# Loading two weight matrices by casting GpSimd transfers in an RWKV-6 and SoLU kernel, with a fused weight preparation, paired decay loads and a new instruction order

## The chip, the cores and the metric

The kernel runs on one core of one Trainium2 chip. The metric is device time in microseconds (us) of one execution, taken as the median over the runs. Each comparison below ran both kernels on the same chip in the same rounds. The kernel before has two speeds: of its 45 timed executions, 25 took 150.9 to 154.1 us and 20 took 154.4 to 160.0 us. The second kind is called slow here. Ratios use fast runs only, and the numbers in square brackets after a ratio are its 95% interval.

Engine names are those of the profile. PE is TensorE, PEld its weight loads, DVE is VectorE, ACT is ScalarE, POOL is GpSimd. SP is SyncE, which issues most transfers. The granted clock is the share of its full clock that TensorE was allowed. SBUF is the on-chip memory; the tiles here lie across up to 128 partitions of it, and an address in it is an offset within a partition. A hold is a tiny copy on GpSimd that waits for a given load, so that what GpSimd issues next waits too (in b_part the second hold waited 2.69 us and w_out was asked for right after it, at 19.43 us).

## The reference

Four batches and eight heads of 768 steps with 48 elements go through a linear attention with decay. Its output, 3072 rows of 384, goes through a layer of 1024 hidden units with a softmax-like gate and a layer norm.

```python
for t in range(S):                        # S = 768
    cur = einsum('bhd,bhe->bhde', u[None] * kt, vt)
    y[:, :, t] = einsum('bhd,bhde->bhe', rt, state + cur)
    state = wt[:, :, :, None] * state + einsum('bhd,bhe->bhde', kt, vt)
x = y.transpose(0, 2, 1, 3).reshape(B * S, H * D)   # 3072 x 384
h = x @ w_in                              # 384 -> 1024
solu = h * softmax(h)
ln = (solu - mean) / sqrt(var + 1e-6) * g_ln
return ln @ w_out                         # 1024 -> 384
```

## The kernel before

The rows are worked off in 24 pieces of 128 (6 chunks of time for each of 4 batches). A text called ORDER fixes the order in which every stage of every piece is issued, and with it the program of each engine. A letter after a word chooses the engine (a, v, g for ACT, DVE, GpSimd). An engine runs its instructions in that order, so one that waits holds back all that stand behind it (in b_part below ACT stood 10.50 us before a scaling that began at 25.64 us, and its next exponential began at 27.60 us). In the lines below p, q, dg and dv are steps of the term with u, kp and kr are k and r scaled and then transposed, vb is v cast to bf16, y is the attention's output, and H, e, he and hq are the hidden layer, its exponential, the product of both and its square.

The inputs r, k, v and w arrive as rows of 48 f32 values, 192 bytes:

```python
def stage(i):
    c, b = units[i]
    L = live[i]
    if name in "kr":
        if "k_and_r" not in L:
            L["k_and_r"] = io.tile([C, 2, H, 64], F32, tag="kr_in", name="kr_in")
        t = L["k_and_r"][:, "kr".index(name)]
    else:
        t = io.tile([C, H, 64], F32, tag=name + "_in", name=name + "_in")
    L[name] = t[:, :, :D]                                  # D = 48 of 64
    sp.dma_start(out=L[name], in_=src[b, :, c * C:(c + 1) * C, :].rearrange("h t d -> t h d"))
```

The weights come as f32 on the queue of SyncE, and are then prepared. Since the layer norm subtracts a mean, the kernel subtracts the mean over the hidden units from the scaled w_out once, and needs no mean for each row:

```python
def load_w_in(j):
    sp.dma_start(out=win_f[:, j, :], in_=win_v[:, j, :])
def load_w_out(half):
    part = slice(half * KF // 2, (half + 1) * KF // 2)
    sp.dma_start(out=wout_f[:, part, :], in_=wout_v[:, part, :])
...
def setup_w_in(j, engine):                 # three casts on ACT
    copy(engine, win_sb[:, j, :], win_f[:, j, :])
def setup_gain(f, engine):                 # gw = w_out * g, eight chunks
    ...
def setup_mean():
    m_ps = small.tile([128, DM], F32, tag="s", name="mean_ps")
    for f in range(KF):
        pe.matmul(m_ps, lhsT=mean_w, rhs=gw[:, f, :], start=(f == 0), stop=(f == KF - 1))
def setup_w2(f, engine):                   # eight additions, all on GpSimd
    engine.tensor_add(out=w2[:, f, :DM], in0=gw[:, f, :], in1=mean_sb)
def log_w(i):                              # one log for each piece
    act.activation(out=L["lw"][:, :, :D], in_=L["w"], func=LN)
```

The softmax here doesn't subtract the row's maximum and nothing guards it: scores larger than these inputs give would overflow.

## Time and profile before

| | before |
|---|---|
| time, median of the first 3 runs | 152.49 us |
| span of the profiled execution (itself a slow one) | 155.2 us |
| busy share: PE, DVE, POOL, ACT | 90%, 83%, 79%, 77% |
| landing of one 192 KB input load, median | 3.8 us (w 4.2) |
| landing of w_out | 23.9 us after the start |
| matmuls issued by 50 us | 512 of 2156 |

The prediction below shows how to read the busy line, the slices, the windows and the chain. The list of transfers gives, for each kind, the number, the size and the median time from issue to landing:

```profile
kr_in<-in_k_dram SPq DMA_DIRECT2D x24, 192.0 KB, 3.8
v_in<-in_v_dram SPq DMA_DIRECT2D x24, 192.0 KB, 3.8
```

The transfer view between 5 and 11 us gives the packets that the queues moved and the time that they took, as a share of 16 engines' time. In that stretch nearly all are rows of 192 bytes (the trace has 94 other packets among them, and 81 to 111 in the other kernels below), so a packet is called a row here:

```profile
DMA packets 6177, 1.17 MB, mean 195 GB/s; under 512 B 6177, under 2 KB 6177, under 8 KB 6177
...
q1 hardware_dynamic: 6177, 1.17, 101.1%
```

16 engines for 6 us are 96 engine-us. 96 times 1.011 over 6177 packets gives 15.7 ns for one row of 192 bytes. A share above 100% means that the times of packets on one engine overlap. Then the time of a row says how long it is under way, and the number of rows says how fast they come.

### The profile page before, as it was taken

The page shows a single profiled execution, that of the slowest core. Times are in us where ns is not written, and L with a number is a line of the kernel's source. Part 1 is how long each engine was busy: PE and PEld are TensorE (multiplying, and loading weights), DVE is VectorE, ACT ScalarE, POOL GpSimd, SP SyncE. Part 2 cuts the span into 40 slices and gives each one's busy share as a digit, 9 for nine tenths or more (in the row PEclk, how much of TensorE's full clock was granted, in tenths as well). Part 3 has the DMA queues.
Part 4 walks back from the last instruction along what each step waited for, and adds up shares of the span by engine and source line. Part 5 has one row for each costly group of instructions (what it writes and reads, how often), then busy time and mean ns, then how long its engine had stood idle before and what let it go on. Part 6 is the DMA issues. An engine that isn't in the chain of part 4 may idle for free.

```text
span 155.2 us, 5295 instructions
## 1 busy us (share of the span) xinstructions
PE 140.4 (90%) x2156; PEld 109.7 (71%) x2156; DVE 129.4 (83%) x231; ACT 120.2 (77%) x232; POOL 123.1 (79%) x152
## 2 busy tenths in 40 slices
PE   6877897699999899999999799939999999999993
PEld 2344584477786787888788587737888778889771
DVE  7546738899998898999976989999889999998661
ACT  4456767989898979798989698829899888895742
POOL 3375965997999799999947999977799899976800
PEclk9999999999999999999999999999999999999999
DMA  4999997989999999899796999999989311011013
GB/s 95 201 185 301 380 303 152 213 160 190 208 202 184 204 229 187 194 205 233 154 205 157 218 217 200 228 250 180 215 196 211 100 51 55 2 55 55 18 62 127
DMA packets 104970, 27.09 MB, mean 175 GB/s; under 512 B 100329, under 2 KB 104562, under 8 KB 104946
## 3 DMA queue, kind: packets, MB, share of 16 engines
q1 hardware_dynamic: 104946, 26.75, 76.4%
q8 instruction: 17, 0.28, 0.7%
q14 instruction: 7, 0.06, 0.1%
HBM read 22.03 MB, written 4.72 MB: 172 GB/s over the span
## 4 chain that ended last, share of the span: by engine, by line
PE 50%; DMA 14%; DVE 10%; SPq 8%; POOL 8%; ACT 4%; issue 3%; POOLq 0%; DVEq 0%
PE o_ps L71 18%; PE h_ps L71 13%; SPq L71 8%; DMA kr_in<-in_k_dram 8%; DMA wout_f<-in_moe_w_out_dram 6%; POOL w L71 5%; PE kr_ps L71 5%; PE cum_ps L71 3%; PE m_ps L71 3%; PE y_ps L71 3%; PE s_ps L71 3%; DVE hq L71 3%; DVE kp L71 2%; PE x_ps L71 2%; DVE he L71 1%
## 5 line engine op out<-in xcount | busy, mean ns | idle before, releaser
L71 PE MATMUL o_ps<-w,he 128*128 128x385 bf16 (+2 forms) x200 | 42.2, 315 | 0.3 <-ACT sq L71 0.3
L71 PE MATMUL h_ps<-xT,win_sb 128*128 128x128 bf16 x576 | 36.0, 219 | 0.1
L71 PEld LDWEIGHTS <-win_sb 128*128 128x128 bf16 x576 | 32.9, 98 | 0.9 <-issue 0.2
L71 PE MATMUL o_ps<-inv_col,e 128*128 128x1 bf16 x192 | 31.1, 165 | 0.0
L71 DVE TENSOR_TENSOR he<-h_ps,e 128x1024 bf16<-128x1024 f32 x24 | 29.2, 1217 | 2.2 <-ACT e L71 2.2
L71 POOL TENSOR_TENSOR hq<-he 128x1024 bf16<-128x1024 bf16 x14 | 26.5, 1895 | 3.7 <-DVE he L71 2.4
L71 ACT ACTIVATE e<-h_ps 128x1024 bf16<-128x1024 f32 x24 | 24.5, 1021 | 6.2 <-PE h_ps L71 6.1
L71 PEld LDWEIGHTS <-he 128*128 128x128 bf16 x208 | 19.7, 96 | 10.5 <-issue 0.3
L71 ACT ACTIVATE cum_ps<-cum_ps 128x772 f32<-128x772 f32 (+1 forms) x24 | 19.2, 801 | 8.8 <-PE cum_ps L71 7.6
L71 DVE TENSOR_TENSOR kp<-cum_ps,kr_in 128x768 bf16<-128x768 f32 x24 | 22.7, 948 | 0.6 <-DMA kr_in<-in_r_dram 0.5
L71 POOL TENSOR_TENSOR q<-p,u_bc 128x384 bf16<-128x384 bf16 x23 | 22.0, 962 | 0.6 <-DVE p L71 0.5
L71 POOL TENSOR_TENSOR p<-kr_in 128x384 bf16<-128x384 f32 x18 | 17.9, 1001 | 5.4 <-DMA kr_in<-in_k_dram 5.4
L71 PEld LDWEIGHTS <-kp 128*128 128x128 bf16 x272 | 17.6, 102 | 4.4 <-DVE kp L71 2.3
L71 POOL TENSOR_TENSOR dv<-vb,dg 128x384 bf16<-128x384 bf16 x22 | 18.2, 830 | 2.3 <-ACT vb L71 1.5
L71 DVE TENSOR_TENSOR m<-m_ps,uts 128x1024 bf16<-128x1024 f32 x14 | 17.0, 1223 | 3.1 <-PE m_ps L71 3.0
L71 PEld LDWEIGHTS <-e 128*128 128x128 bf16 x192 | 18.3, 96 | 0.1
L71 PE MATMUL kr_ps<-ident,kp 128*128 128x128 bf16 x192 | 15.9, 230 | 1.4 <-DVE kp L71 1.4
L71 PEld LDWEIGHTS <-kr 64*128 64x128 bf16 (+1 forms) x272 | 10.7, 98 | 4.9 <-DVE kr L71 2.2
L71 ACT ACTIVATE lw<-w_in 128x384 bf16<-128x384 f32 x23 | 11.7, 523 | 2.7 <-DMA w_in<-in_w_dram 2.7
L71 ACT COPY kr<-kr_ps 128x1024 bf16<-128x1024 bf16 x13 | 13.2, 1014 | 0.5 <-PE kr_ps L71 0.4
L71 POOL TENSOR_SCALAR_AFFINE_SELECT m<-m 128x1024 bf16<-128x1024 bf16 x10 | 11.0, 1103 | 2.5 <-ACT m L71 2.4
L71 PE MATMUL cum_ps<-lw,uti_neg 128*128 128x384 bf16 x24 | 8.3, 347 | 4.8 <-DVE kp L71 3.3
(93 smaller groups left out, 284.3 us busy)
## 6 DMA issues: line engine op xcount, KB each, us to landing
w_in<-in_w_dram SPq DMA_DIRECT2D x24, 192.0 KB, 4.2
kr_in<-in_r_dram SPq DMA_DIRECT2D x24, 192.0 KB, 3.8
kr_in<-in_k_dram SPq DMA_DIRECT2D x24, 192.0 KB, 3.8
v_in<-in_v_dram SPq DMA_DIRECT2D x24, 192.0 KB, 3.8
out_dram<-o SPq DMA_DIRECT2D x23, 192.0 KB, 3.1
win_f<-in_moe_w_in_dram SPq DMA_DIRECT2D x3, 512.0 KB, 6.1
wout_f<-in_moe_w_out_dram SPq DMA_DIRECT2D x2, 768.0 KB, 8.8
out_dram<-o SPq DMA_DIRECT2D x2, 96.0 KB, 1.6
```

The lines of the kernel that those rows point to most:

```text
L71: made = make(*args, **kwargs)
```

## The change

The intent is to take work off the compute engines before the first output: GpSimd's transfers cast w_in on the way, each group of weights is held back until a given load has landed so that the first inputs go first, w_out is centred and scaled in one DVE operation for half of it, and w with its log is taken in pairs. The core of the diff:

```diff
 ORDER = """          # all of it replaced; weights as iwin0..2, iwout0..1
+            elif name == "w":
+                if i % 2 == 0:
+                    t2 = io.tile([C, 2, H, 64], F32, tag="w_in", name="w_in", bufs=4)
+                    ...
+                if i >= 4:
+                    sp.dma_start(out=L["w2_in"]..., in_=src[b:b + 2, ...])   # two batches in one
-    win_f = consts.tile([128, KM, DF], F32)
+    win_sb = consts.tile([128, KM, DF], BF16)
-    wout_f = consts.tile([128, KF, DM], F32)
+    wout_f = consts.tile([128, KF, DM], F32R)
+    seen = consts.tile([1, 4], F32)
+    def after(loaded):
+        n_seen.append(1)
+        pool.tensor_copy(out=seen[:, len(n_seen):len(n_seen) + 1], in_=loaded)
     def load_w_in(j):
-        sp.dma_start(out=win_f[:, j, :], in_=win_v[:, j, :])
+        if j == 0:
+            after(live[2]["w"][:1, 0, :1])
+        pool.dma_start(out=win_sb[:, j, :], in_=win_v[:, j, :])
     def load_w_out(half):
+        if half == 0:
+            after(win_sb[:1, 1, :1])
         ...
-        sp.dma_start(out=wout_f[:, part, :], in_=wout_v[:, part, :])
+        pool.dma_start(out=wout_f[:, part, :], in_=wout_v[:, part, :])
-    mean_w = consts.tile([128, 128], BF16)
-    gw = consts.tile([128, KF, DM], BF16)
+    g_wide = consts.tile([128, KF, 128], F32R)
     def setup_mean(half):
+            pe.matmul(live[0]["mean_ps"], lhsT=g_wide[:, f, :], rhs=wout_f[:, f, :], ...)
     def setup_w2(f, engine):
-        engine.tensor_add(out=w2[:, f, :DM], in0=gw[:, f, :], in1=mean_sb)
+        if "scaled" in live[f]:
+            engine.tensor_add(out=w2[:, f, :DM], in0=w2[:, f, :DM], in1=mean_sb)
+        else:
+            engine.scalar_tensor_tensor(out=w2[:, f, :DM], in0=wout_f[:, f, :].bitcast(F32),
+                                        scalar=gr[:, f:f + 1], in1=mean_sb, op0=MULT, op1=ALU.add)
     ...                # pairs of w in log_w, constants set up in another order
```

## The prediction

The forecast's sum: 3 us from 20 to 50 us, 1 us in the first 20 and 1 to 2 us from 85 to 105, together taken as about 5 us off 152.5, so 147.5 us. The fall of GpSimd's busy time to 115 us never had the transfers in it. Rival (b) rests on the one long square in the trace (4.09 us against 0.68), and rival (c) blamed the holds, stacked with a time for each GpSimd transfer.

> **What bounds the kernel now.** I read the page's summary and slices first, then busy time by stage, then the chain of waits, then single tiles. From the page:
>
> ```profile
> PE 140.4 (90%) x2156; PEld 109.7 (71%) x2156; DVE 129.4 (83%) x231; ACT 120.2 (77%) x232; POOL 123.1 (79%) x152
> ...
> PE   6877897699999899999999799939999999999993
> ...
> DMA  4999997989999999899796999999989311011013
> ```
>
> TensorE is the fullest engine, but all four compute engines are above 75%, and the DMA engines are full from about 5 to 120 us. So an average settles nothing; the stages do. The windows view, one row for each stretch that I chose (busy us, and in brackets the number of instructions):
>
> ```profile
> 0.00:20.00 20.00, 15.19 (x105) 8.39 (x105) 12.94 (x47) 11.23 (x14) 11.63 (x23) 1.00 0.92 237
> 20.00:30.00 10.00, 7.75 (x98) 5.74 (x96) 6.91 (x13) 7.79 (x14) 7.06 (x8) 1.00 0.95 213
> 30.00:50.00 20.00, 19.29 (x309) 15.26 (x308) 18.87 (x31) 17.30 (x34) 18.61 (x24) 1.00 0.95 191
> 50.00:85.00 35.00, 34.60 (x603) 28.75 (x601) 30.62 (x50) 31.05 (x65) 30.27 (x44) 1.00 0.94 195
> 85.00:105.00 20.00, 16.23 (x270) 13.12 (x268) 18.32 (x25) 13.99 (x27) 19.02 (x20) 1.00 0.99 223
> 105.00:150.00 45.00, 44.59 (x766) 36.69 (x763) 40.49 (x66) 37.24 (x77) 36.48 (x37) 1.00 0.41 100
> ```
>
> Columns: PE, weight load, DVE, ACT, POOL, granted clock, DMA share, GB/s. The busy time of PE flatters it, so I count matmuls. In 50 to 85 us it does 603 in 35 us, 17.2 a us; 105 to 150 us has 17.0. I take 17.2 as its full pace. What each stage lacks is its length less its count over 17.2: 0 to 20 us lacks 13.9 us, 20 to 30 us lacks 4.3, 30 to 50 us lacks 2.0, 85 to 105 us lacks 4.3. The end (150 to 155.2 us, 21 matmuls) lacks 4.0. So PE is the bound from about 50 us on, and some 28 us are lost, two thirds of them in the first 30 us. A check from the chain view: one batch of 128 rows costs PE h 1.36, o 0.75 and 0.94, kr 0.47, m 0.33, y 0.39, x 0.18, cum 0.41, s 0.34, together 5.17 us; 24 of them are 124 us, and 124 + 28 is 152, near the span of 155.2 us. (The profiled execution was slower than the timed ones, median 152.49 us; I take the shape from the profile and the level from the times.)
>
> The chain in order of time shows what fills the early loss (start, us, what):
>
> ```profile
> 13.97 9.87 DMA wout_f<-in_moe_w_out_dram
> ...
> 23.87 1.12 ACT gw L71 x2
> ...
> 26.31 0.38 ACT mean_sb L71
> 26.69 0.07 issue
> 26.75 7.75 POOL w L71 x8
> ...
> 39.74 4.45 DMA kr_in<-in_k_dram
> ```
>
> The weights arrive at 23.9 us. They are then scaled, averaged on PE, copied, and GpSimd spends 7.75 us adding the mean eight times. Its own p, q and dv queue up behind that. They free the input buffers, so the DMA of k for later batches is issued late, twice 4.5 us in this chain, and the chain gets back to PE only at 53 us.
>
> The late hole (85 to 105 us) has one large cause, seen in DVE's timeline:
>
> ```profile
> 98.25 4.09 DVE L71 TENSOR_TENSOR hq<-he 128x1024 bf16<-128x1024 bf16 x1
> ```
>
> and on PE, at the end of it:
>
> ```profile
> 103.26 0.34 PE L71 MATMUL cum_ps<-lw,uti_neg 128*128 128x384 bf16 x1 [2.71 <-DVE kp L71]
> ```
>
> The same square took 0.68 us at 40.94 us. Here GpSimd ran q, dv and two p back to back beside it (98.18 to 101.78 us), the square ended 0.6 us later, and PE stood 2.71 us behind.
>
> [...]
>
> **The change part by part.** Counts are from the two lists of operations, durations from the groups by form.
> - w_in cast in the transfer: three casts of 1.05 us leave ACT (3.1 us), at 15.7 to 20.0 us. PE began h at 20.06 us, 0.06 us after the last of them, so up to 1 us of this is on the path. Three transfers of GpSimd come instead, and two for w_out. [...]
> - w_out: before, two scalings on GpSimd (2.5 us), four on ACT, two on DVE, and eight additions on GpSimd (7.75 us). After, four scalings on ACT as before, four additions on GpSimd (3.9 us), and on DVE four that scale and add at once (about 0.55 us each as f32 of 384, 2.2 us). The mean no longer waits for the scaling: g is spread into a 128x1024 tile on ACT (about 1.05 us) and multiplies w_out as it is. From landing to the last addition was 34.5 less 23.9, 10.6 us. I expect some 2 us for mean and copy and 4 us for four additions on each of two engines: 6 us, a gain of 4.5 us for GpSimd. [...]
> - The holding back: the weights start only after w of batch 2 and w_out after w_in, so inputs of four batches share the DMA with less. Weights may land 1 to 2 us later than 23.9 us; the bytes of w_out are the same.
> - w in pairs: twenty logs of 0.52 us become ten of about 0.84 us (the slope from 384 to 1024 elements in the casts and logs is 0.82 ns): 2.1 us off ACT. Ten transfers fewer to issue. The rows stay 192 bytes, so the DMA does the same.
> - The order of all work and engines is new as well. Sums: hq GpSimd 14 to 9, ACT 5 to 8, DVE 5 to 7; kr ACT 13 to 7, DVE 11 to 17; v casts on ACT 6 to 2; masks on GpSimd 10 to 12; halvings there 6 to 9. With these, ACT falls by about 5.6 us to 114.6, DVE rises by about 1 us to 130.4, GpSimd falls by about 8 us to 115 [...]. [...]
>
> On the path: of the 4.3 us lacking in 20 to 30 us and the 2.0 in 30 to 50 us I give back 3. In the first 20 us more batches have their inputs early, 1 us. In 85 to 105 us a lighter GpSimd and another order give back 1 to 2 us, by luck as much as by design. Together about 5 us off 152.5.
>
> **Rivals.** (a) DMA takes over: it is already 0.95 full to 105 us, at 195 GB/s with 192-byte rows. If only the DMA sets when batches come, freeing engines moves nothing and the time stays at 151 to 153. For it: the two waits for k in the chain, and 13.9 us lost at the start. Against it: the share falls to 0.41 after 105 us, so the loads finish 30 us before the end and PE is the one behind. (b) [...] DVE now has seven squares, two v casts and four additions [...]. Two more stalls like the one of 3.4 us would cost 5 us and leave 150 to 154. For it, DVE is the second fullest engine; against it, GpSimd has five squares of 1.9 us fewer. (c) Weights arrive too late [...]: landing at 28 us rather than 24 would eat the 4 us, result 151 to 153. (d) The new order fits so well that PE runs closed from 20 us: 20 + 124 less 6 already done + 4 of end = 142.
>
> **Range and chances.** 5 us off gives 147.5 us. (d) sets the low side, 143.5, (a) to (c) the high side, 151.5. Faster by over 2% means under about 149.4: 0.70. One of the rivals holding all of the gain: 0.24. Two of them together: 0.06.
>
> **What would show it.** No win casts on ACT; the last addition to w_out by about 31 us rather than 34.5; 20 to 50 us with more matmuls than the 407 of before; ACT near 115 and GpSimd near 115 us busy; PE from 50 us at 17 a us. It would be wrong if w_out lands after 27 us, if the float32r matmuls take over 0.4 us each, if DVE squares again take 4 us, or if PE waits for k or w after 50 us.

## The result and the profile after

The changed kernel is correct. It takes 162.14 us (median of 4 runs, 161.08 to 163.51) against 152.18 us for the kernel before (4 runs, 150.94 to 152.75). The ratio of fast runs is 1.0643, 95% interval 1.0539 to 1.0748. A ratio is the mean time of one kernel's fast runs over the mean of the other's fast runs of the same rounds, so it isn't quite the ratio of the medians.

The page of the changed kernel, busy times and two rows of the slices:

```profile
PE 141.8 (88%) x2156; PEld 111.3 (69%) x2157; DVE 127.2 (79%) x236; ACT 115.7 (72%) x218; POOL 118.0 (73%) x157
...
PE   6786248996999999989999989699899999999991
...
DMA  4999999999999999999999999999999991111022
...
kr_in<-in_k_dram SPq DMA_DIRECT2D x24, 192.0 KB, 5.1
...
v_in<-in_v_dram SPq DMA_DIRECT2D x24, 192.0 KB, 5.4
```

Every compute engine but PE has less work (predicted for ACT and GpSimd; DVE was to have 1 us more), and the kernel is 6% slower. The DMA row is full for 33 slices of 4.02 us, to about 133 us. Before it was full for 31 slices of 3.88 us, to about 120 us. The loads of 192 KB land in 5.1 and 5.4 us rather than 3.8. The windows view of the changed kernel, with the columns of the prediction (PE, weight load, DVE, ACT, POOL, granted clock, DMA share, GB/s):

```profile
0.00:20.00 20.00, 12.62 (x92) 6.86 (x94) 10.64 (x43) 9.73 (x13) 9.44 (x21) 0.99 1.23 162
20.00:30.00 10.00, 7.26 (x61) 5.54 (x60) 5.80 (x11) 1.21 (x3) 6.20 (x10) 0.51 1.21 220
30.00:50.00 20.00, 17.85 (x268) 14.02 (x266) 18.49 (x29) 16.77 (x30) 15.51 (x16) 1.00 1.23 177
...
85.00:105.00 20.00, 18.15 (x302) 14.64 (x300) 15.48 (x27) 15.98 (x32) 15.79 (x21) 1.00 1.13 184
```

PE has issued 421 matmuls by 50 us (92 + 61 + 268) against 512 before (527 in the fast profile of b_swq below). The DMA share is above 1.1 where it was 0.92 to 0.99, and in three of the four stretches fewer bytes move than before. Between 5 and 11 us, in the transfer view:

```profile
DMA packets 5236, 0.99 MB, mean 165 GB/s; under 512 B 5236, under 2 KB 5236, under 8 KB 5236
...
q1 hardware_dynamic: 5236, 0.99, 152.3%
```

The same kind of row now takes 96 times 1.523 over 5236, 27.9 ns instead of 15.7. Since these times overlap, the pace falls by less: 5236 rows in 6 us instead of 6177, 15% fewer. Over the whole run the mean of all 98304 rows in the trace is 21.3 ns instead of 15.6. The first transfer of GpSimd is issued only at 11.76 us, so it can't be the weights that slow these. The rest of the kernel then waits for inputs, which the chain of waits in order of time shows (start, us, what):

```profile
14.50 8.13 DMA kr_in<-in_r_dram
...
60.59 6.96 DMA kr_in<-in_k_dram
...
91.65 6.63 DMA v_in<-in_v_dram
```

A second thing went further than foreseen. GpSimd's timeline shows when the weights were asked for (start, us, engine, operation, and in brackets the idle time before it):

```profile
11.40 0.41 POOL L72 COPY seen<-w_in 1x1 f32<-1x1 f32 x1 [2.31 <-DMA w_in<-in_w_dram]
...
20.63 0.50 POOL L72 CAST vb<-v_in 128x384 bf16<-128x384 f32 x1 [3.01 <-DMA v_in<-in_v_dram]
21.08 0.59 POOL L72 DMA_DIRECT2D win_sb<-in_moe_w_in_dram  x1
...
22.47 0.18 POOL L72 CAST seen<-win_sb 1x1 f32<-1x1 bf16 x1
22.59 1.57 POOL L72 DMA_DIRECT2D wout_f<-in_moe_w_out_dram  x2
```

The second hold itself (the copy at 22.47 us) waited for nothing. What kept w_out back was the cast of v at 20.63 us, which stood ahead of the third part of w_in, and so of w_out, in GpSimd's own program. The halves of w_out landed 8.0 and 10.0 us after their issue, the second at 33.4 us instead of 23.9.

### The profile page after: what moved, and what is told of

The parts are those of the page before. It is cut to its first block, busy times and chain, and to the rows that moved or that the text cites. A ratio compares the mean times of both kernels' runs of the same rounds, so it can differ in the third digit from the quotient of the medians.

```text
span 160.8 us, 5277 instructions
## 1 busy us (share of the span) xinstructions
PE 141.8 (88%) x2156; PEld 111.3 (69%) x2157; DVE 127.2 (79%) x236; ACT 115.7 (72%) x218; POOL 118.0 (73%) x157
## 4 chain that ended last, share of the span: by engine, by line
PE 48%; DMA 17%; DVE 11%; SPq 10%; issue 4%; ACT 3%; POOL 3%; DVEq 0%; ACTq 0%; POOLq 0%
PE o_ps L72 16%; PE h_ps L72 13%; SPq L72 10%; DMA kr_in<-in_r_dram 5%; DMA kr_in<-in_k_dram 4%; DMA v_in<-in_v_dram 4%; PE kr_ps L72 4%; PE y_ps L72 3%; PE cum_ps L72 3%; DMA out_dram<-o 3%; DVE kp L72 3%; PE m_ps L72 3%; PE s_ps L72 3%; ACT cum_ps L72 2%; PE x_ps L72 2%
## 5 line engine op out<-in xcount | busy, mean ns | idle before, releaser
L72 PE MATMUL h_ps<-xT,win_sb 128*128 128x128 bf16 x576 | 37.3, 224 | 0.3 <-DVE kp L72 0.3
L72 PEld LDWEIGHTS <-win_sb 128*128 128x128 bf16 x576 | 34.1, 100 | 2.0 <-issue 0.9
L72 POOL TENSOR_TENSOR hq<-he 128x1024 bf16<-128x1024 bf16 x9 | 17.0, 1892 | 9.9 <-DVE he L72 8.7
L72 POOL TENSOR_TENSOR q<-p,u_bc 128x384 bf16<-128x384 bf16 x23 | 21.8, 951 | 1.6 <-DVE p L72 1.0
L72 POOL TENSOR_TENSOR p<-kr_in 128x384 bf16<-128x384 f32 x20 | 19.9, 1000 | 4.0 <-DMA kr_in<-in_r_dram 4.0
L72 POOL TENSOR_TENSOR dv<-vb,dg 128x384 bf16<-128x384 bf16 x23 | 19.4, 842 | 2.9 <-DVE dg L72 1.5
L72 POOL CAST vb<-v_in 128x384 bf16<-128x384 f32 x20 | 10.2, 508 | 7.2 <-DMA v_in<-in_v_dram 4.9
L72 DVE TENSOR_TENSOR m<-m_ps,uts 128x1024 bf16<-128x1024 f32 x12 | 14.6, 1219 | 0.7 <-PE m_ps L72 0.4
L72 POOL TENSOR_SCALAR_AFFINE_SELECT m<-m 128x1024 bf16<-128x1024 bf16 x12 | 13.2, 1096 | 2.6 <-ACT m L72 2.4
L72 DVE COPY kr<-kr_ps 128x1024 bf16<-128x1024 bf16 x17 | 11.7, 688 | 3.1 <-PE kr_ps L72 3.1
L72 PEld LDWEIGHTS <-kr 64*128 64x128 bf16 (+1 forms) x272 | 10.6, 96 | 4.8 <-DVE kr L72 1.5
L72 ACT ACTIVATE o<-o_ps,rs 128x384 f32<-128x384 f32 x20 | 11.6, 578 | 2.8 <-DMA out_dram<-o 2.6
```

The source lines that it names most:

```text
L72: made = make(*args, **kwargs)
```

## The experiments

Fourteen runs of thirteen kernels were made (a_al64b repeats a_al64). All gave a correct result. The texts name theories by letters. A letter belongs to its own text.

### The rows that cross a 256-byte line

What differs for an input load, when its code is the same? The place of its tile. The change removes three tiles and adds others, and the input tiles, which the compiler places behind the constants, moved from offset 93504 to offset 78944 in each partition (offsets of the built programs; the traces don't show them). Rows lie 256 bytes apart, so all rows of all tiles start at the same place past a multiple of 256: at 64 before and at 96 after. A row of 192 bytes from 64 ends exactly at the next multiple. From 96 every row crosses it. That such a row takes longer is a guess, which the runs below test.

A filler tile, never read, ahead of the input tiles moves them, and with them the output and work tiles, all by the same number of bytes. The constants and the order of work stay. **a_al64** puts the changed kernel's rows back at 64:

```diff
     live = [dict() for _ in units]
+    shift = io.tile([C, 56], F32, tag="shift", name="shift", bufs=1)     # 224 bytes
+    nc.vector.memset(shift, 0.0)
```

> The changed kernel with a 224-byte filler tile ahead of the input tiles, so that they start at 64 modulo 256 as in the kernel before, not at 96. Theory 1 (where a 192-byte row lands in SBUF sets the transfer rate: 32 off a 64-byte line is slow): 5 to 14 us back from 163 to about 200 GB/s, DMA share from 1.54 to about 1.0, loads land in 3.8 us again, time 144 to 149 us. Theory 2 (the mere presence of GpSimd's transfers slows all others): no change, 161 to 163 us. Theory 3 (the new order is bad by itself): rate back or not, the time stays above 156 us.

Measured: 154.7 us (154.09 to 155.16), ratio 1.0101 [1.0031, 1.017]. The transfer view from 5 to 11 us:

```profile
DMA packets 6694, 1.26 MB, mean 211 GB/s; under 512 B 6694, under 2 KB 6694, under 8 KB 6694
...
q1 hardware_dynamic: 6694, 1.26, 106.8%
```

That is 15.3 ns a row. Some 5 of the 6.4 per cent are gone with a filler of 224 bytes. The rate came back as theory 1 said; the 144 to 149 us that it gave did not come. **b_mis32** does the reverse: the kernel before, moved to 96 by a filler of 32 bytes (`[C, 8]` in the same two lines).

> The kernel before with a 32-byte filler tile ahead of the input tiles: they start at 96 modulo 256 as in the changed kernel. Theory 1: rate at 5 to 14 us falls from 204 to about 163 GB/s, DMA share about 1.5, time 158 to 166 us. Theories 2 and 3: 152 us, unchanged.

Measured: 164.88 us (164.64 to 165.74), ratio 1.0778 [1.0703, 1.0853].

```profile
DMA packets 5310, 1.00 MB, mean 167 GB/s; under 512 B 5310, under 2 KB 5310, under 8 KB 5310
...
q1 hardware_dynamic: 5310, 1.00, 147.0%
```

26.6 ns a row. The kernel before, with no other change than the place of its tiles, becomes at least as slow as the changed kernel. This settles the cause of most of the loss. That the work tiles moved too doesn't explain it: GpSimd's square took 1.89 us and DVE's he 1.22 us on average in before, b_mis32, after and a_al64 alike.

**b_swq** tests a rival: that a transfer issued by GpSimd anywhere slows the other queue. It lets GpSimd load the 4 KB of gains in the kernel before.

```diff
-        sp.dma_start(out=g_rows, in_=moe_g_ln.rearrange("(ko ki) -> ko ki", ki=128))
+        pool.dma_start(out=g_rows, in_=moe_g_ln.rearrange("(ko ki) -> ko ki", ki=128))
```

> The kernel before with only the 4 KB transfer of the gain rows issued by GpSimd, so that a software-fed queue is in use. Theory 2: DMA share above 1.3 and rate about 165 GB/s from 5 us on, time 158 us or more. Theories 1 and 3: 152 us, unchanged.

Measured: 155.66 us median of a mixture (152.67 to 157.99), ratio of the fast runs 1.0014 [0.9889, 1.0139]. From 5 to 11 us a row took 15.3 ns. The rival falls, also by a_al64, which has all five weight transfers of GpSimd. This run also gave what the kernel before lacked, a profile of a fast execution, and I use it below as the measure of a good start:

```profile
30.00:50.00 20.00, 19.51 (x319) 15.48 (x318) 18.78 (x28) 17.28 (x34) 18.41 (x24) 1.00 0.96 192
```

With 113 and 95 before it, that is 527 matmuls by 50 us.

Is it the crossing, or an odd start? **a_al128** (filler 32 bytes) puts the changed kernel's rows at 128, a round start from which every row crosses. **a_al32** (filler 192 bytes) puts them at 32, a less round start from which no row crosses.

> The changed kernel with a 32-byte filler: input tiles start at 128 modulo 256, on a 64-byte line, but each 192-byte row crosses a 256-byte line. If theory 1 holds with 64-byte lines: as fast as at 64 modulo 256. If it holds with 256-byte lines instead: as slow as now, 160 to 163 us. Theory 2: unchanged, 162 us.

> The changed kernel with a 192-byte filler: input tiles start at 32 modulo 256, off a 64-byte line, but no 192-byte row crosses a 256-byte line (32 to 224). If crossing a 256-byte line is what costs: as fast as a_al64, about 154.7 us, and about 195 GB/s at 5 to 14 us. If lying off a 64-byte line costs as well: 160 to 163 us and about 165 GB/s.

Measured: a_al128 162.87 us (162.45 to 163.22), ratio 1.0632 [1.0547, 1.0716]. a_al32 155.12 us (154.16 to 155.27, 5 rounds), ratio 1.0151 [1.009, 1.0211]. The crossing decides, not the roundness. **b_al0** (the kernel before, filler 192 bytes, start 0) asks whether a start on the line is better still, that is, whether the bytes between the line and the start of a row cost time too.

> The kernel before with the input rows moved from 64 to 0 past a 256-byte line by a 192-byte filler; nothing else. Theory C (only a crossing of a 256-byte line costs): no row crosses in either, so the ratio is 1.00 within 0.7% and 5 to 14 us shows about 200 GB/s at a share near 1.0. Rival B (what counts is the bytes from the line below the start to the end of the row, 192 here against 256 before): each row then costs a quarter less, 5 to 14 us moves 230 GB/s or more, and the kernel is 1 to 2% faster, since its DMA is full till 120 us.

Measured: 153.65 us median of a mixture (152.88 to 157.88), ratio of fast runs 1.0041 [0.9947, 1.0135], so the same. All starts side by side, the ns worked out as above from the transfer view between 5 and 11 us:

| kernel | start past the line | crosses | rows in 6 us, share | ns a row | ratio to before |
|---|---|---|---|---|---|
| b_al0 | 0 | no | 7035, 111.6% | 15.2 | 1.004 |
| a_al32 | 32 | no | 6602, 107.3% | 15.6 | 1.015 |
| before | 64 | no | 6177, 101.1% | 15.7 | 1 |
| a_al64 | 64 | no | 6694, 106.8% | 15.3 | 1.010 |
| b_mis32 | 96 | yes | 5310, 147.0% | 26.6 | 1.078 |
| after | 96 | yes | 5236, 152.3% | 27.9 | 1.064 |
| a_al128 | 128 | yes | 5341, 140.0% | 25.2 | 1.063 |

In this stretch rows that do not cross take 15.2 to 15.7 ns wherever they start, and rows that cross take 25.2 to 27.9 ns (over the whole runs, from the traces, 15.6 to 15.8 and 21.0 to 21.8 ns). In 6 us 6177 to 7035 rows move without a crossing, and 5236 to 5341 with it. So the time goes with whether a row crosses, and does not rise evenly with the start from 0 to 128. Why a crossing costs, the traces don't show. One sign of the rival did appear: b_al0 moved 244 GB/s from 5 to 14 us, above the 230 that it had named. But from 11 us on the larger packets of the weights are among them (194 of 549 packets between 11 and 14 us are over 2 KB), and from 5 to 11 us, where hardly anything but rows moves, the higher rate goes with a higher share, the time for one row hardly falls (15.2 against 15.7 ns), and the kernel's doesn't. (Its profile is of a slow execution, as that of before is.)

### What the aligned changed kernel still loses

With the rows in place, 1% remains. **a_al64b** repeats a_al64 with more rounds:

> The same kernel as a_al64, for comparison on this chip: all theories 154 to 155.5 us, 1.0 to 1.5% over the fast runs of the kernel before.

Measured: 155.27 us (153.73 to 156.75), ratio 1.0118 [1.004, 1.0196]. Both intervals leave out 1, so the 1% against the fast runs is real. (Over all runs of those rounds, slow ones too, the medians are 154.7 against 154.1 us and 155.3 against 153.7 us.) Its place is seen in the windows of a_al64:

```profile
20.00:30.00 10.00, 8.63 (x110) 6.90 (x109) 8.54 (x15) 4.26 (x7) 6.84 (x10) 0.81 1.20 277
30.00:50.00 20.00, 17.84 (x267) 13.88 (x266) 19.12 (x30) 16.98 (x32) 16.20 (x19) 1.00 1.00 201
```

With 92 before, it has 469 matmuls at 50 us, 58 fewer than 527. From 50 us on it runs at full pace (614 in the next 35 us). 58 over 17.2 a us is 3.4 us, of which the time shows 1.5 to 1.8 us (the two ratios). All further kernels of the new order carry the filler of a_al64.

**a_nohold** takes both holds away and leaves the order as it is:

```diff
-        if j == 0:
-            after(live[2]["w"][:1, 0, :1])
         ...
-        if half == 0:
-            after(win_sb[:1, 1, :1])
```

> Aligned as in a_al64, without the two reads that hold the weight transfers back; the order is kept. Theory H (the holds make w_out late, 31.4 us in a_al64): w_out lands before 28 us and the time is 150 to 153 us. Theory Q (GpSimd's in-order queue makes it late: the third part of w_in waits behind the cast of v of batch 1): w_out still lands at about 30 us or later and the time stays at 154 to 155 us.

Measured: 156.07 us (155.26 to 157.02), ratio 1.0239 [1.0173, 1.0305]. w_out is issued at 20.2 and 21.0 us, only 1.1 us earlier than with the holds (21.3 and 22.2 us in a_al64). The holds are not the main reason why it is late. Its place in GpSimd's program is. The time is above what both theories gave, and without the holds the kernel is some 1.2% slower than with them, so they seem to earn something (the intervals overlap a little). **a_early** therefore also moves all five weight transfers ahead in that program:

```diff
-exp1 ldv1 iwin0 dm1 M0 lw2 ldr3 iwin1 ...
+exp1 ldv1 iwin0 iwin1 iwin2 iwout0 iwout1 dm1 M0 lw2 ldr3 ...
```

> Aligned, no holds, and all five weight transfers issued by GpSimd one after another where the first was. Theories H and Q: w_out lands at 21 to 25 us, the additions end by about 30 us and the time is 147 to 151 us. Rival (the inputs of the first batches then share the DMA with the weights and come later, so nothing is won): w_out early, but v of batch 1 lands after 20 us and the time stays at 153 us or more.

Measured: 160.92 us (159.65 to 162.68), ratio 1.0529 [1.0424, 1.0635]. w_out lands at 19.9 and 22.5 us, some nine us earlier than in a_al64 (28.6 and 31.4 us), and the kernel loses 5%. The waits of a_early say why (who waited, for whom, us in total, times, longest):

```profile
ACT vb L72 <- DMA v_in<-in_v_dram: 6.3, 1, 6.3
...
PE y_ps L72 <- ACT vb L72: 4.7, 1, 4.7
```

The weights took the DMA. These waits are for v of the first piece, which landed at 19.8 us, 11 us after its issue (13.0 us in a_al64), and PE stood behind it. v of the second piece landed at 24.4 us (19.0 us in a_al64). In 20 to 30 us PE issues 51 matmuls. **a_mid** seeks the middle: the holds stay, and only v of the second piece and the weights change places.

```diff
-... lw1 ldv0 ldw3 ...   ldv1 iwin0 ... iwin1 ...   sel1 vb1g ... iwin2 ... iwout0 ... iwout1
+... lw1 ldv0 ldv1 ldw3 ...   iwin0 ... iwin1 iwin2 ...   sel1 iwout0 iwout1 vb1g ...
```

> Aligned as in a_al64, both holds kept, but the third part of w_in and the two of w_out are issued by GpSimd ahead of its cast of v of batch 1, and v of batch 1 is loaded ahead of w and k of batch 3. If late weights are what the aligned kernel still loses (w_out landed at 31.4 us there, 23.9 us in the kernel before): w_out lands at 25 to 28 us, 30 to 50 us has over 290 matmuls instead of 267, and the time is 149 to 152 us. If an early weight transfer again takes the rate from the inputs, as in a_early: v of batch 1 later than 19 us and 154 us or more.

Measured: 160.39 us (157.6 to 163.2), ratio 1.0327 [1.0207, 1.0448] from only two fast runs, and its profile is of a slow one. It has 36 matmuls in 20 to 30 us. In that profile w_out landed at 25.6 us and v of the second piece at 18.5 us, as its first theory asked, and the gain didn't come. I take no more from it.

**a_hw** keeps the new order and the pairs, and returns the weights to the old way: f32 on the queue of SyncE at the same places, casts of w_in on ACT, scaling on ACT and DVE, mean in bf16.

```diff
-        pool.dma_start(out=win_sb[:, j, :], in_=win_v[:, j, :])
+        sp.dma_start(out=win_f[:, j, :], in_=win_v[:, j, :])
...
-        pool.dma_start(out=wout_f[:, part, :], in_=wout_v[:, part, :])
+        sp.dma_start(out=wout_f[:, part, :], in_=wout_v[:, part, :])
```

> Aligned, the new order and the pairs kept, but the weights come as f32 by the sync queue at the same places, are cast by ScalarE, scaled by ScalarE and VectorE, averaged, and added in place, as in the kernel before. If fetching the weights through GpSimd is what costs the aligned kernel its gain: w_out lands at about 25 us, 20 to 50 us has over 400 matmuls instead of 377, time 149 to 152 us. If the new order itself is what is lost: 154 us or more. DMA rate with inputs in both cases near 200 GB/s.

Measured: 156.66 us (155.97 to 157.5), ratio 1.0234 [1.0173, 1.0296]. With early weights prepared in the old way, the new order does worse: 240 matmuls in 30 to 50 us against 267. The halves of w_out landed at 23.7 and 25.8 us, but ACT's first scaling began only at 29.5 us, without waiting for them.

**a_single** takes the pairs apart, one load and one log for each piece:

```diff
-                    sp.dma_start(out=L["w2_in"]..., in_=src[b:b + 2, ...])
+                    for a in range(2):
+                        sp.dma_start(out=live[i + a]["w"], in_=src[b + a, ...])
```

> Aligned as in a_al64, but w comes in single transfers with single logs for all batches, at the places of the pairs. If pairing is worth what I forecast (2.1 us of ScalarE, off the path): ACT busy up by about 2 us and the time within 0.7 us of a_al64. If larger transfers matter for the queue: 1 us or more slower.

Measured: 155.69 us (154.27 to 156.89), ratio 1.0177 [1.0091, 1.0264]. Against 1.0101 and 1.0118 with the pairs, they may be worth half a per cent. The intervals overlap, so this is inconclusive.

**b_part** turns the question round: the old order with the weights alone handled as in the change (casting GpSimd transfers, both holds, wide gain, float32r mean, four chunks in one DVE operation), rows at 64 by a filler.

```diff
-ldwin2 ... ldwin1 ... win2a ... win1a ... ldwin0 ... win0a ... ldwout0 ... gw1a gw0a ... gw4v gw6v gw3g ... gw2g mean
+ldwin2 ... ldwin1 ... ldwin0 ... ldwout0 ... gw1a gw0a ... gm:a ... mean      # transfers by GpSimd, with the holds
-wt2g wt3g wt4g wt6g
+wt2v wt3v wt4v wt6v                                                            # scale and add in one
```

> The kernel before, its order, single loads and single logs kept and its rows at 64 past a line, with the weights alone as in the change: casting GpSimd transfers with both holds, wide gain, float32r mean, four chunks of w_out scaled by ACT and added to on GpSimd, four scaled and added in one DVE operation. Theory N (what the aligned changed kernel still loses is the new order): within 1% of before or faster by up to 1.5%, 150.5 to 154 us, and over 500 matmuls by 50 us. Theory W (the fetch of the weights by GpSimd costs it): w_out lands at 28 us or later, under 490 matmuls by 50 us, 154 to 157 us.

Measured: 161.22 us (160.66 to 162.56), ratio 1.0582 [1.0499, 1.0665]. w_out landed at 29.3 us, and 357 matmuls were issued by 50 us, as theory W had it, but the time is above the 154 to 157 us that W gave. Theory N falls. Here is the view that shows what happened, ACT's first scalings of w_out in its timeline, in b_part:

```profile
25.64 1.12 ACT L71 ACTIVATE w<-wout_f,gr 128x384 bf16<-128x384 f32 x2 [10.50 <-DMA wout_f<-in_moe_w_out_dram]
```

and in the kernel before:

```profile
21.07 1.12 ACT L71 ACTIVATE gw<-wout_f,gr 128x384 bf16<-128x384 f32 x2 [1.06 <-DMA wout_f<-in_moe_w_out_dram]
```

In the old order ACT comes to the scaling early. It used to wait 1.06 us there (1.07 us in the fast profile of b_swq). In b_part the first half of w_out lands 4.6 us later, and ACT comes there 4.9 us sooner, at 15.1 us instead of 20.0, since its casts of w_in are gone. So it stands for 10.50 us with all its exponentials and logs queued behind. GpSimd's timeline gives the reason for the lateness (w_out asked for at 19.4 and 22.1 us, against 13.3 and 14.0 before):

```profile
16.03 0.59 POOL L71 DMA_DIRECT2D win_sb<-in_moe_w_in_dram  x1
19.31 0.18 POOL L71 CAST seen<-win_sb 1x1 f32<-1x1 bf16 x1 [2.69 <-DMA win_sb<-in_moe_w_in_dram]
19.43 0.75 POOL L71 DMA_DIRECT2D wout_f<-in_moe_w_out_dram  x1
...
22.14 0.81 POOL L71 DMA_DIRECT2D wout_f<-in_moe_w_out_dram  x1
```

Here the second hold did wait, 2.69 us, and the second half of w_out stood behind a p and a q as well. So order and weights go together. With the late weights the new order and its pairs cost 1.1% where the old order costs 5.8%: the new one puts the scalings behind other work of ACT. With the weights in the old way it costs 2.3% (a_hw), and makes no use of their being early: there w_out has landed by 25.8 us, and ACT comes to it at 29.5 us. That this is why it costs is my reading; no run took it alone. (In a_early it is 22.5 and 34.5 us, but late inputs held ACT up there too.)

**b_split** asks whether the gain that I had credited to a lighter GpSimd existed at all. It is the kernel before with four of the eight additions moved from GpSimd to DVE, and no GpSimd transfer. It was also the version that seemed most likely to beat both kernels.

```diff
-wt2g ... wt3g ... wt4g ... wt6g
+wt2v ... wt3v ... wt4v ... wt6v
```

> The kernel before, word for word, with four of the eight additions to w_out (chunks 2, 3, 4, 6) moved from GpSimd to DVE, the one part of the change's idea that needs no GpSimd transfer. Theory P (the 7.75 us chain of additions on GpSimd was worth what the prediction took for it): GpSimd has about 3.9 us less in 26 to 35 us, 30 to 50 us does more than 324 matmuls, and the kernel is 1 to 2% faster. Rival Q (the DMA sets the pace of the first 50 us[...]): ratio 1.00 within 0.7%.

Measured: 154.56 us (154.0 to 155.98), ratio 1.0145 [1.0078, 1.0212]: slower by 1 to 2%, which neither theory gave. The windows, the additions, and GpSimd's timeline in b_split, in three views, and then GpSimd's timeline in b_swq, the fast profile of the old order:

```profile
30.00:50.00 20.00, 18.75 (x288) 14.73 (x289) 17.89 (x31) 15.36 (x28) 11.90 (x15) 0.91 0.96 193
```

```profile
L71 DVE TENSOR_TENSOR w<-gw,mean_sb x4: 343/840/1062, 26.3 to 31.7; 128x384 bf16<-128x384 bf16 x4
```

```profile
25.80 4.07 POOL L71 TENSOR_TENSOR w<-gw,mean_sb 128x384 bf16<-128x384 bf16 x4
33.43 0.96 POOL L71 TENSOR_TENSOR q<-p,u_bc 128x384 bf16<-128x384 bf16 x1 [3.56 <-DVE p L71]
```

```profile
25.80 7.74 POOL L71 TENSOR_TENSOR w<-gw,mean_sb 128x384 bf16<-128x384 bf16 x8
33.51 0.91 POOL L71 TENSOR_TENSOR q<-p,u_bc 128x384 bf16<-128x384 bf16 x1
```

GpSimd is done with its additions at 29.9 us, against 33.5 in b_swq, and then waits 3.56 us for DVE's p, which stands behind the additions that DVE took over. They took 0.84 us each in the median (minimum, median and maximum are given in ns), though the one at 31.7 us, after GpSimd had finished its own, took 0.34. GpSimd's next work starts at 33.43 us instead of 33.51, so nothing is won there. (Against the slow profile of before, 34.46 us, it would look like a gain of one us.) And DVE has paid: its kp starts at 30.00 us instead of 27.92, behind two additions of 2.04 us, and PE waits 2.37 us for that kp, about the size of the loss (2.2 us).

### The account at 50 us

The count of matmuls at 50 us, taken from the windows view, goes with the loss of the kernels with rows in place. The second column of numbers is (527 less the count) over 17.2; the third is the ratio less 1, times 152.7 us, about the mean of the fast runs of before over all rounds. The count is rough: the slow profiles of before and of b_al0, which cost the same, have 512 and 538, which is 1.5 us apart.

| kernel | matmuls by 50 us | behind, us | measured loss, us |
|---|---|---|---|
| b_split | 489 | 2.2 | 2.2 |
| a_al32 | 486 | 2.4 | 2.3 |
| a_al64 | 469 | 3.4 | 1.5 |
| a_nohold | 467 | 3.5 | 3.6 |
| a_al64b | 461 | 3.8 | 1.8 |
| a_single | 454 | 4.2 | 2.7 |
| a_hw | 438 | 5.2 | 3.6 |
| a_early | 388 | 8.1 | 8.1 |
| b_part | 357 | 9.9 | 8.9 |
| after (rows cross) | 421 | 6.2 | 9.8 |

Of the kernels of the new order a_al64, a_al64b, a_single and a_hw win back 1.5 to 2.0 us later, and a_al32, a_nohold and a_early nothing. a_mid is left out, since its profile is slow. The granted clock doesn't order the list: it is 1.00 up to 50 us in a_early, which has 388, and 0.70 to 20 us in b_swq, which has 527. The changed kernel with its crossing rows loses more after 50 us, since its inputs stay late (302 matmuls in 85 to 105 us against 338 in b_swq).

No version beat the kernel before. The best of the changed ones is the one with the filler, 1.0 to 1.2% slower.

## Why the prediction was wrong

It gave 147.5 us, with 143.5 to 151.5 as the range, and the kernel takes 162.14 us.

**The step that failed first** is "The rows stay 192 bytes, so the DMA does the same." The rows stayed, their place did not. I looked at what the loads are and not at where their tiles come to lie once other tiles are removed. This is worth 5 to 5.5 of the 6.4 per cent (1.0643 less 1.0101 or 1.0118). Rival (a), which said that the DMA sets the pace, was near, but its worst case was no change. It had no way to make the DMA slower.

**The second** is "Weights may land 1 to 2 us later than 23.9 us". The second half of w_out landed at 33.4 us, 9.5 us later. Even with aligned rows it was 31.4 us. Rival (c) named the direction, and 28 us as its threshold. The cause that it named, stacked holds, was the smaller part: without holds, w_out was issued at 20.2 us, 1.1 us sooner. GpSimd's own order is the larger part, a transfer behind a cast that waits for v. The cost in the old order, where the hold waited 2.69 us, is 5.8% (b_part).

**The third** is the credit: "I expect some 2 us for mean and copy and 4 us for four additions on each of two engines: 6 us, a gain of 4.5 us for GpSimd." In the changed kernel the last of them, on DVE, ended at 41.8 us. The prediction had said 31. From landing it took 8.4 us rather than 6 (10.6 before). The one-operation form took 0.94 us in the median, where I had 0.55, as the tile view of the changed kernel shows:

```profile
L72 PE MATMUL mean_ps<-wout_f,g_wide x8: 333/336/420, 32.8 to 34.1; 128*128 128x384 f32 x8
...
L72 DVE SCALAR_TENSOR_TENSOR w<-wout_f,gr,mean_sb x4: 621/940/1266, 36.2 to 41.1; 128x384 bf16<-128x384 f32 x4
```

And b_split shows that such a gain for GpSimd isn't a gain for the end: its share of 4 us became a wait of 3.56 us for DVE.

**The fourth** is the 1 to 2 us that the stretch from 85 to 105 us was to give back. The 4.3 us lacking there were read from a slow profile, and taken off a level of fast runs. In the fast profile of b_swq the old order issues 338 matmuls in this stretch, not 270, which is its full pace: there was nothing to give back.

Of the four signs of being wrong that the prediction named, two came: w_out landed after 27 us, and after 50 us the chain waits for inputs (k at 60.59 us). From 20 to 50 us there were 329 matmuls, where it asked for more than 407.

**Right:** the work that ACT and GpSimd were to lose. ACT came to 115.7 us (said: 114.6), GpSimd to 118.0 (115, transfers not counted). DVE came to 127.2 us (130.4), a fall of 2.2 us where a rise of 1 was said; the stall of 3.4 us in the slow profile was part of its 129.4. The casts of w_in are gone. A log of two pieces takes 0.842 us (0.84). A transfer took GpSimd 0.55 to 0.82 us to issue. DVE's squares take at most 1.56 us, so the stall of 4 us did not return. The float32r mean wasn't slow in the changed kernel: eight matmuls began within 1.3 us (32.8 to 34.1), 336 ns each in the median, as the eight in bf16 did before (23.7 to 25.0, 326 ns); in b_part the median was 484 ns. But none of these set the end. The prediction counted the busy time of ACT and GpSimd well, and misread what the inputs and the in-order queues would do with it.

**Open:** which placements in the new order cost the last 1%. Why the kernel before has slow runs: its slow profile has the 4.09 us square at 98 us and the fast one of b_swq doesn't (1.43 us at most), but no run took that cause alone. Whether the pairs are worth anything. No run took the old order with the one-operation form and early float32r weights.

## What to carry to other kernels

When a change removes or adds a tile, look at where the other tiles come to lie: in this kernel rows of 192 bytes that crossed a multiple of 256 cost 5 to 8%, and a filler of 224 bytes took that back. Other lengths of row were not tried. When an early transfer moves to a compute engine's queue, it gets that engine's waits (w_out was asked for at 22.6 us rather than 13.3), and an in-order consumer that was placed for the old arrival will stand (1.06 us became 10.50). Before crediting work taken off one engine, ask who has to do it and who stands in line behind it there.
